# A mixture-of-experts kernel: the second expert's second matrix is split before the branch behind the routing, and part of a dense matrix is decoded beside the first products

## The chip, the cores and the metric

One core of a Trainium2 chip runs the whole program. The metric is the device time of one execution in microseconds, lower is better. The engines have one queue each and run it in order: PE (TensorE matmuls; PEld is its weight load), DVE (VectorE), ACT (ScalarE), POOL (GpSimd) and SP, which here only issues DMAs. Engines wait for each other through semaphores.

## The reference, cut to what matters

```python
x = attention(r, k, v, w, u)                    # linear attention, 3072 tokens x 384
logits = x @ w_gate                             # 8 experts, each takes exactly 384 tokens
order = argsort(-logits.flatten())              # greedy: best (token, expert) pairs first
for e in range(8):
    h = maximum(x[mask_e] @ moe_w1[e], 0)       # 384 -> 1024
    y[mask_e] = h @ moe_w2[e]                   # 1024 -> 384
h = maximum(maximum(y @ v1, y @ v2), y @ v3)    # three dense 384 x 768 matrices
out = h @ w_out                                 # 768 -> 384
```

`moe_w1`, `moe_w2` are float32 for each expert; the dense matrices `v1`, `v2`, `v3` and `w_out` come as float64 and are read as pairs of 32-bit words.

## The kernel before, in words

Three stages follow each other: the attention (until about 165 us of the profiled span), the routing (until about 197 us), and the eight experts (until the end). Every product of the experts is made from float16 halves: a matrix is split into a high and a low half, scaled by a power of two, and a product is the three passes high x high, low x high, high x low.

**Preparing a matrix** is work of ACT and DVE and is cut into small pieces. `weight(e, which)` (from line 634 on) gives the pieces of one expert matrix: four `look`s (ACT squares and sums a part of the staged matrix, line 617), `collect`, `share`, `done` (some 13 tiny DVE instructions that find the scale, lines 666, 430 to 436, 454 to 468), and five to seven `split`s (ACT writes a high half, line 684, and DVE the low half of the part before, line 688). `double(i)` (from line 707 on) gives those of a dense matrix: for each of three parts `shift`, `low`, `sign` decode float64 bits to float32 (ACT line 724, DVE lines 739, 746, 755), then the sums, `collect`, `share`, `done`, and four `split`s (ACT 780, DVE 783). `V[2]` is the third dense matrix, called V3 below, and `WO` is the last one, 384 wide.

**The planner** `Feed` holds all these pieces in one list. Under it are the stage blocks: 768 KB loads by SP into four rotating tiles (`SLOTS` is 4); `ahead()` issues a block's load when its first use is at most `AHEAD` = 6 pieces away and its tile is free. `run()` issues the next piece. `take(tag, budget)` runs pieces while its account `spare` is over 0.3; `spare` is the smaller of zero and what it was, plus the budget, and each piece run by anyone lowers it by the cost written beside the piece. A debt is kept. All of this is decided when the program is made; on the chip there are only the queues.

**Where the pieces go.** `plan()` makes the list for what remains after the attention: W2[1] (expert 1's second matrix), V3, WO, then expert 2's matrices and so on. `aside(n)` in the routing's rounds runs four pieces there, the looks of W2[1]. `settle()` ends the routing: it computes the token lists `ids` and a flag, and every engine loads the flag. `then()` issues the gather of expert 0's tokens (three indirect DMAs by POOL, line 861). Then comes a branch on every engine (`tc.If(bad != 0)`, line 1407): if the routing needs more rounds, its body runs; it doesn't here, so it is jumped over. Behind the branch the experts' PSUM and SBUF pools take over the room of the routing's pools.

`Experts.run()` (from line 1010 on) issues the experts' work in a fixed order: `gather(1)`, `first(0)` with its first five column blocks computed token slice by token slice as the gather lands (PE transposes a slice, line 886; ACT and DVE write its halves, lines 895 and 896; PE multiplies, line 904), `second(0)`, `first(1)`, `second(1)`, then for each expert `third` (six groups of three products, the dense V matrices; ACT and DVE take the maximum, lines 977 and 979) and `fourth` (WO, line 997; store by POOL, line 1002). Between products `side(time)` calls `take()` with a budget from the pieces that remain and the time until they are due; `flush(tag)` issues whatever a stage still needs, `flush(1)` V3 before `third(0)`, `flush(1.5)` WO before `fourth(0)`.

The calls around the routing's end:

```python
bad = self.settle()
then()
for _ in other:
    pass
self.aside = lambda pieces: None
with tc.If(bad != 0) as _:
```

Of the kernel before, what the change touches and what calls it, by code (L numbers as in the profile page):

```python
# [44 lines left out]
class Attention:  # L45
# [270 lines left out]
    def run(self, feed):  # L316
        nc = self.nc
        self.load(3)
        feed.ahead(2)
        for i in range(2):  # L320
            self.turn(i)
        self.scores(0)
        self.extra(0)
        for i in range(NT):
            if i == 2:
                self.routing.prepare()

            def side(j):
                if i:
                    feed.spare = 0.0  # L330
                    feed.take(9, min(0.9, feed.due((4 * (i - 1) + j) / (4 * (NT - 4)))), j)

            self.load(i + 4)
            self.across(i + 3)
            self.store(i - 1)
            self.decayed(i + 2)
            self.natural(i + 3)
            self.bonus(i + 2)
            side(1)
            self.turn(i + 2)  # L340
            self.fade(i - 1)
            side(2)
            self.scores(i + 1)
            self.extra(i + 1)
            side(3)
            self.cross(i - 1)
            self.keep(KEEP)
            self.rows(i)
            self.gate(i - 2)
            side(4)  # L350
            self.state(i)
        while feed.left(9):
            feed.run()
        self.store(NT - 1)
        self.gate(NT - 2)
        self.cross(NT - 1)
        self.gate(NT - 1)
        K = self.K
        nc.scalar.activation(K.raw, self.lg, AF.Copy, scale=-1.0)
# [137 lines left out]
class Feed:  # L497
# [30 lines left out]
    def close(self):  # L528
# [7 lines left out]
            self.items.append((tag, f, pe))  # L536
        self.plan = []

    def ahead(self, most=99):
        while self.loaded < min(most, len(self.blocks)):  # L540
            b, n = self.blocks[self.loaded], self.loaded - self.SLOTS
            free = n < 0 or self.blocks[n].last < self.at - 1
            must = b.first <= self.at
            if not must and not (free and b.first <= self.at + self.AHEAD):
                break
            b.load()
            self.loaded += 1
# [38 lines left out]
class Experts:  # L586
# [243 lines left out]
    def plan(self, late):  # L830

        feed = self.feed = Feed()
        self.early = False
        parts = [(0.2, self.weight(1, 1), None)] + [(1, self.double(i), 0) for i in late]
        parts[-1] = (1, parts[-1][1] + [(self.common, False, [], 1.5)], None)
        parts.append((1.5, self.double(3), 0))
        for e in range(2, E):
            parts += [(e, self.weight(e, 0), 7), (e + 0.3, self.weight(e, 1), 6)]
        feed.chain(parts)
        feed.close()  # L840
        feed.ahead(Feed.SLOTS)

    def open(self, ctx):
        tc = self.tc
# [65 lines left out]
            return self.psum.tile([128, CAP], F32, name="pg", bufs=3)  # L910
        return self.psum.tile([128, CAP], F32, name="ps", bufs=2)

    def first(self, e, wide=False, ahead=0):

        nc = self.nc
        h = self.act.tile([128, 2, self.KF, CAP], F16, name="ht", bufs=1)
        self.HT[e] = h
        w = self.W1[e][0]
        ps = [self.bank(f, wide) for f in range(ahead)]
        if ahead:  # L920
            for a, _ in enumerate(self.turn(e, True)):
                for f in range(ahead):
                    self.product(ps[f], w, slice(f * 128, f * 128 + 128), self.XT[e], self.KD,
                                 slice(a * 128, a * 128 + 128))
        for f in range(self.KF):
            if f < ahead:
                p = ps[f]
            else:
                p = self.bank(f, wide)
                self.product(p, w, slice(f * 128, f * 128 + 128), self.XT[e], self.KD)  # L930
            nc.scalar.activation(h[:, 0, f], p, AF.Relu)  # L931
            nc.vector.scalar_tensor_tensor(h[:, 1, f], p, 0.0, h[:, 0, f], op0=OP.max, op1=OP.subtract)  # L932
            yield
# [77 lines left out]
    def run(self):  # L1011
        nc, self.stores, feed = self.nc, [], self.feed
        F1, F2, G1, G2 = 1.45, 3.87, 4.36, 2.9
        ahead, turn = 8 * F1 + 3 * F2, 6 * G1 + 3 * G2
        clock, limit = [0.0], [1]
        room = {F1: 1.05, F2: 3.6, G1 / 3: 1.3, G2: 2.7}

        def due(tag):

            if tag < 2:  # L1020
                return ahead + 8 * F1 if tag < 1 else 2 * ahead + (6 * G1 if tag > 1 else 0.0)
            return 2 * ahead + turn + (int(tag) - 2) * (ahead + turn) + (8 * F1 + 5 * G1 if tag > int(tag) else 0.0)

        tags = sorted({item[0] for item in feed.items}, key=due)

        def side(time, part=1.0):

            clock[0] += time
            pace = max((feed.rest(tag) / max(due(tag) - clock[0] - SLACK[0] - SLACK[1] * feed.waits(tag), time) for tag in tags
                        if tag <= limit[0] and feed.left(tag)), default=0.0)  # L1030
            feed.take(limit[0], min(SLACK[2] * pace * time, part * room[time]), None, time, APART)

        def go(units, time=0):
            for _ in units:
                if time:
                    side(time)

        def flush(tag):
            while feed.rest(tag):
                feed.run()  # L1040

        self.gather(1)
        first = self.first(0, True, 5)
        for _ in range(5):
            next(first)
            clock[0] += F1
        self.gather(2)
        go(first, F1)
        go(self.turn(1))
        soon = self.second(0, lambda j: side(F2))  # L1050

        def step():
            if soon:
                soon.pop(0)()

        step()
        first = self.first(1, True)
        for f in range(self.KF):
            next(first)
            side(F1, 0.5 if soon else 1.0)  # L1060
            step()
        next(first, None)
        flush(0.2)
        soon = self.second(1, lambda j: side(F2))
        flush(1)
        limit[0] = 99
        for e in range(E):
            n = e + 1
            third, fourth = self.third(e, 0, self.KG, lambda: side(G1 / 3)), self.fourth(e)
            first = self.first(n) if e and n < E else iter(())  # L1070
            if e:
                flush(n)
            for g in range(4):
                next(third)
                step()
                side(G1 / 3, 0.6)
                if g == 1:
                    go(self.turn(e + 2))
                    self.gather(e + 3)
                for _ in range(2):  # L1080
                    if next(first, self) is not self:
                        side(F1)
            next(third)
            step()
            side(G1 / 3, 0.6)
            if e and n < E:
                flush(n + 0.3)
                soon = self.second(n, lambda j: side(F2))
                step()
            next(third)  # L1090
            step()
            side(G1 / 3, 0.6)
            flush(1.5)
            for a in range(3):
                next(fourth)
                step()
                step()
                side(G2)


class Routing:
# [291 lines left out]
    def run(self, ctx, other, aside, scales, then):  # L1393

        tc = self.tc
        self.other, self.aside = other, aside
        self.work = ctx.enter_context(tc.tile_pool(name="rwork", bufs=2))
        self.psum = ctx.enter_context(tc.tile_pool(name="psum_r", bufs=1, space=PSUM))
        scales.psum = lambda: self.psum.tile([128, 512], F32, name="px")
        for n in range(self.ROUNDS):  # L1400
            self.round(self.nl if n else self.K.raw, 6 if n == 0 else 4, n)
        bad = self.settle()
        then()
        for _ in other:
            pass
        self.aside = lambda pieces: None
        with tc.If(bad != 0) as _:
            self.more(self.MORE)
            then()
# [84 lines left out]
```

## Time and profile before

| what | value |
|---|---|
| median of the runs | 697.07 us |
| lowest and highest of three | 695.23 and 697.87 us |
| the profiled execution | 701.96 us |
| its span in the profile | 700.2 us |
| PE busy | 648.9 us, 93% |
| DVE busy | 402.0 us, 57% |
| ACT busy | 351.6 us, 50% |
| POOL busy | 238.0 us, 34% |

The span is the time from the first to the last instruction of the profiled execution. A busy share is a mean over stages with different limits; in the page's 40 slices PE is fullest from the fourteenth on, where slices of 17.5 us read 9 tenths or 8, and thinnest around the routing. The granted clock of PE is read in the same slices: 9 is full speed, 5 or 6 about half of it.

### The profile page before, as it was taken

What the parts mean: (1) busy time and instruction counts of PE and PEld (TensorE: products, weight loads), DVE (VectorE), ACT (ScalarE), POOL (GpSimd) and SP (SyncE); (2) the same over time, 40 slices, a digit from 0 to 9 for tenths busy, and PEclk for the clock granted to TensorE, in tenths of its full rate; (3) what the DMA queues carried; (4) which work ended last, traced back from release to release, by engine and by line L of the source; (5) the groups of instructions that cost most, each with busy time, mean ns of one, the idle gap of its engine ahead of it and who ended that gap; (6) DMA issues with size and microseconds to landing.
All of it is one profiled execution on the core that took longest, in us unless ns stands there. A gap on an engine that the chain in (4) does not pass through costs nothing.

```text
span 700.2 us, 14403 instructions
## 1 busy us (share of the span) xinstructions
PE 648.9 (93%) x5663; PEld 431.1 (62%) x5663; DVE 402.0 (57%) x1068; ACT 351.6 (50%) x785; POOL 238.0 (34%) x264
## 2 busy tenths in 40 slices
PE   5999998997589998699999999999999999999996
PEld 4788787886366555356666656666665666666663
DVE  7667997784734959636466544735636552551321
ACT  3576467643324645565466446545454635442321
POOL 6989999980050003123123112202212110210222
PEclk9889999996569999899999999999999999999999
DMA  7877866613033524227234410620611130000000
GB/s 226 268 230 226 276 215 199 212 47 113 2 95 67 205 90 110 94 79 141 64 124 64 141 45 35 158 91 35 157 47 69 40 96 1 35 0 1 35 1 34
DMA packets 54762, 72.97 MB, mean 104 GB/s; under 512 B 21408, under 2 KB 42016, under 8 KB 54688
## 3 DMA queue, kind: packets, MB, share of 16 engines
q1 hardware_dynamic: 51616, 62.55, 29.0%
q0 software_dynamic: 3072, 9.44, 4.9%
q8 instruction: 46, 0.75, 0.4%
q14 instruction: 28, 0.23, 0.1%
HBM read 58.41 MB, written 9.44 MB: 97 GB/s over the span
## 4 chain that ended last, share of the span: by engine, by line
PE 53%; issue 8%; DVE 5%; ACT 4%; POOL 1%; ACTq 0%; POOLq 0%; DVEq 0%
PE pg L904 25%; PE ps L904 20%; PE px L997 8%; ACT w L684 1%; DVE top L979 1%; POOL gt L984 1%; ACT junk L617 1%; DVE da L746 1%; DVE x2s L960 0%; ACT gt L983 0%; DVE ht L932 0%; DVE v L783 0%; DVE sc L430 0%; DVE da L739 0%; POOL out_dram L1002 0%
## 5 line engine op out<-in xcount | busy, mean ns | idle before, releaser
L904 PE MATMUL pg<-x2s,v 128*128 128x384 f16 x1296 | 218.2, 326 | 5.3 <-ACT top L977 3.2
L904 PEld LDWEIGHTS <-v 128*128 128x128 f16 x1296 | 126.6, 98 | 90.9 <-issue 6.0
L984 POOL TENSOR_TENSOR gt<-top,gt 128x384 f16<-128x384 f32 x48 | 44.5, 928 | 349.2 <-ACT gt L983 295.5
L904 PEld LDWEIGHTS <-w 128*128 128x128 f16 x1242 | 116.9, 99 | 75.1 <-issue 3.7
L688 DVE SCALAR_TENSOR_TENSOR w<-stage,sc,w 128x512 f16<-128x512 f32 (+1 forms) x80 | 71.6, 920 | 57.6 <-ACT w L684 57.6
L979 DVE SCALAR_TENSOR_TENSOR top<-pg,sc,top 128x384 f32<-128x384 f32 x96 | 59.0, 615 | 74.6 <-PE pg L904 63.7
L904 PE MATMUL ps<-ht,w 128*128 128x384 f16 x576 | 94.9, 326 | 1.6 <-DVE ht L932 1.6
L904 PE MATMUL ps<-xt,w 128*128 128x384 f16 (+1 forms) x540 | 88.3, 317 | 0.2 <-ACT xt L895 0.2
L997 PE MATMUL px<-wo,gt 128*128 128x384 f16 x432 | 75.0, 333 | 6.3 <-DVE wo L783 2.4
L983 ACT ACTIVATE gt<-top 128x384 f16<-128x384 f32 x48 | 25.1, 522 | 109.7 <-DVE top L979 109.7
L997 PEld LDWEIGHTS <-gt 128*128 128x128 f16 x432 | 42.7, 100 | 37.4 <-issue 7.9
L684 ACT ACTIVATE w<-stage,sc 128x512 f16<-128x512 f32 (+1 forms) x80 | 61.4, 798 | 2.2 <-DVE sc L468 2.2
L617 ACT ACTIVATE junk<-stage 128x768 bf16<-128x768 f32 x64 | 53.7, 838 | 7.2 <-DMA stage<-in_moe_w_dram 6.2
L932 DVE SCALAR_TENSOR_TENSOR ht<-ps,ht 128x384 f16<-128x384 f32 x56 | 30.9, 554 | 32.5 <-ACT ht L931 32.4
L1002 POOL DMA_INDIRECT out_dram<-o,ids x24 | 23.9, 996 | 46.0 <-ACT o L1000 46.0
L977 ACT ACTIVATE top<-pg,sc 128x384 f32<-128x384 f32 x48 | 27.6, 576 | 20.1 <-PE pg L904 17.5
L230 DVE TENSOR_TENSOR am<-pA,mask 128x512 f32<-128x512 f32 x48 | 30.7, 680 | 10.6 <-PE pA L227 10.6
L943 ACT ACTIVATE x<-ps 128x384 f32<-128x384 f32 x24 | 11.7, 490 | 46.4 <-PE ps L904 46.4
L931 ACT ACTIVATE ht<-ps 128x384 f16<-128x384 f32 x56 | 26.8, 481 | 15.7 <-PE ps L904 15.2
L227 PE MATMUL pA<-rt,kt 64*128 64x128 f32 x384 | 31.0, 297 | 2.5 <-DVE am L230 2.2
L1000 ACT ACTIVATE o<-px,sc 128x384 f32<-128x384 f32 x24 | 13.9, 580 | 38.1 <-PE px L997 34.8
L129 POOL TENSOR_TENSOR rt<-rt,tr 128x512 f32<-128x512 f32 x22 | 32.2, 1464 | 1.5 <-DMA rt<-in_rt_dram 1.5
(231 smaller groups left out, 873.6 us busy)
## 6 DMA issues: line engine op xcount, KB each, us to landing
stage<-in_moe_w_dram SPq DMA_DIRECT2D x41, 768.0 KB, 5.7
kn<-in_k_dram SPq DMA_DIRECT2D x24, 192.0 KB, 4.7
rn<-in_r_dram SPq DMA_DIRECT2D x24, 192.0 KB, 5.2
v<-in_v_dram SPq DMA_DIRECT2D x24, 192.0 KB, 3.3
rt<-in_rt_dram SPq DMA_DIRECT2D x48, 96.0 KB, 3.3
x_rows<-x SPq DMA_DIRECT2D x24, 192.0 KB, 2.6
stage<-in_moe_w_out_dram SPq DMA_DIRECT2D x3, 768.0 KB, 4.8
xg<-x_rows,ids POOLq DMA_INDIRECT x24, 4.7
```

What stands on the lines that cost most here:

```text
L129: (engine or self.nc.gpsimd).tensor_mul(self.RT[i], self.RT[i], self.tr)
L227: nc.tensor.matmul(pa[s][:, j, :], kt[FULL[s], j * C:(j + 1) * C], rt[FULL[s], j * C:(j + 1) * C], start=True, stop=True, skip_group_check ...
L230: nc.vector.tensor_mul(am[:, s], pa[s], self.mask[:, None, :].to_broadcast([128, NP, C]))
L617: self.nc.scalar.activation(self.K.junk, x, AF.Square, accum_out=total)
L684: nc.scalar.activation(hi, raw, AF.Copy, scale=st["s"])
L688: nc.vector.scalar_tensor_tensor(lo, raw, st["s"], hi, op0=OP.mult, op1=OP.subtract)
L904: nc.tensor.matmul(p[:, rows], w[:, wi, k, cols], x[:, xi, k, rows], start=k == 0 and wi + xi == 0, stop=k == kb - 1 and xi == 1, skip_gro ...
L932: nc.vector.scalar_tensor_tensor(h[:, 1, f], p, 0.0, h[:, 0, f], op0=OP.max, op1=OP.subtract)
L977: nc.scalar.activation(t, p, AF.Copy, scale=self.ratio[i])
L979: nc.vector.scalar_tensor_tensor(t, p, self.ratio[i], top, op0=OP.mult, op1=OP.max)
L984: nc.gpsimd.tensor_sub(gt[:, 1, g], top, gt[:, 0, g])
L997: nc.tensor.matmul(p, gt[:, gi, g, a * 128:(a + 1) * 128], self.WO[:, wi, g, :], start=g == 0 and gi + wi == 0, stop=g == self.KG - 1 and ...
```

## The change

Four things change.

1. In `plan()` the four first stage blocks are loaded at once (`fill()`), where `ahead()` would stop at the first block that is not needed within six pieces. Two of the four belong to V3.
2. Behind `then()`, and ahead of the branch, eight pieces run: W2[1]'s `collect`, `share`, `done` and its five `split`s.
3. In `first(0)`, `between` runs five pieces behind the second token slice's products and two behind the third's: V3's decode up to the second part's `sign`.
4. The due time by which the planner paces WO is three V groups earlier (`3 * G1` for `6 * G1`).

```diff
+    def fill(self):
+        while self.loaded < min(self.SLOTS, len(self.blocks)):
+            self.blocks[self.loaded].load()
+            self.loaded += 1
+
@@ plan
-        feed.ahead(Feed.SLOTS)
+        feed.fill()
@@ first
-    def first(self, e, wide=False, ahead=0):
+    def first(self, e, wide=False, ahead=0, between=lambda a: None):
...
                     self.product(ps[f], w, slice(f * 128, f * 128 + 128), self.XT[e], self.KD,
                                  slice(a * 128, a * 128 + 128))
+                between(a)
@@ Experts.run
-                return ahead + 8 * F1 if tag < 1 else 2 * ahead + (6 * G1 if tag > 1 else 0.0)
+                return ahead + 8 * F1 if tag < 1 else 2 * ahead + (3 * G1 if tag > 1 else 0.0)
...
-        first = self.first(0, True, 5)
+        first = self.first(0, True, 5, lambda a: self.aside((0, 5, 2)[a]))
@@ Routing.run
         for _ in other:
             pass
+        self.aside(8)
         self.aside = lambda pieces: None
         with tc.If(bad != 0) as _:
```

## Rows read from the trace of the kernel before

**Rows 1.** Page, part 1 (PE) and part 5 (the looks and sums)

```profile
PE 648.9 (93%) x5663; PEld 431.1 (62%) x5663; DVE 402.0 (57%) x1068; ACT 351.6 (50%) x785; POOL 238.0 (34%) x264
...
L617 ACT ACTIVATE junk<-stage 128x768 bf16<-128x768 f32 x64 | 53.7, 838 | 7.2 <-DMA stage<-in_moe_w_dram 6.2
```

**Rows 2.** Windows: PE, PEld, DVE, ACT, POOL busy, clock, DMA share, GB/s

```profile
280.00:300.00 20.00, 14.57 (x73) 7.59 (x71) 12.95 (x44) 10.12 (x20) 3.87 (x6) 0.83 0.23 84
```

**Rows 3.** Line 1407, the branch; durations ns min/median/max, first and last start

```profile
L1407 DVEq EVENT_SEMAPHORE  x2: 21/21/21, 200.9 to 201.0; - x2
L1407 PEldq EVENT_SEMAPHORE  x2: 51/51/51, 201.5 to 201.7; - x2
...
L1407 PEldq COMPARE_BRANCH  x1: 3648/3648/3648, 197.8 to 197.8; - x1
L1407 DVEq COMPARE_BRANCH  x1: 72/72/72, 197.9 to 197.9; - x1
```

**Rows 4.** Waits of SP, 190 to 212 us: total, times, longest

```profile
SPq L878 <- DVEq L1407: 7.9, 1, 7.9
```

**Rows 5.** Timeline from the branch to the first products: start, duration, instruction

```profile
202.13 1.51 PE L886 MATMUL px<-identf,xg 128*128 128x128 f32 x6 [1.56 <-PEq L1407]
203.16 1.09 ACT L895 ACTIVATE xt<-px,sc 128x384 f16<-128x384 f32 x2 [7.41 <-issue]
...
203.79 1.13 PE L904 MATMUL ps<-xt,w 128*128 128x128 f16 x9 [0.15 <-ACT xt L895]
...
208.56 0.27 PE L904 MATMUL pg<-xt,w 128*128 128x128 f16 x2 [1.07 <-issue]
```

**Rows 6.** Windows at the clock's two rises; the second line: PE alone

```profile
204.00:206.00 2.00, 2.00 (x24) 1.98 (x23) 0.92 (x2) 0.26 (x1) 1.60 (x2) 0.58 0.62 169
...
297.00:298.00 1.00, 1.00 (x5) 0.58 0.00 0
```

**Rows 7.** Timeline of W2[1]'s pieces, 221 to 232 us

```profile
221.24 0.15 DVE L666 TENSOR_REDUCE sc<-wpeak 128x1 f32<-128x4 f32 x1
...
223.77 0.22 DVE L468 TENSOR_SCALAR sc<-sc 128x1 int32<-128x1 int32 x2
...
227.27 3.40 ACT L684 ACTIVATE w<-stage,sc 128x768 f16<-128x768 f32 x4
228.24 3.81 DVE L688 SCALAR_TENSOR_TENSOR w<-stage,sc,w 128x768 f16<-128x768 f32 x4 [4.26 <-ACT w L684]
```

**Rows 8.** Timeline: one V3 piece on DVE, and second(1) on PE

```profile
240.64 0.95 DVE L746 SCALAR_TENSOR_TENSOR da<-stage,da 128x768 int32<-128x768 int32 x1
...
243.63 11.86 PE L904 MATMUL ps<-ht,w 128*128 128x384 f16 x72 [1.65 <-DVE ht L932]
```

**Rows 9.** Timeline: V3's scale, its splits and the first maximum

```profile
250.66 0.15 DVE L765 TENSOR_REDUCE sc<-peaks 128x1 f32<-128x3 f32 x1 [2.96 <-ACT junk L617]
...
256.38 2.58 ACT L780 ACTIVATE v<-wo,sc 128x768 f16<-128x768 f32 x3
...
260.85 0.58 ACT L977 ACTIVATE top<-pg,sc 128x384 f32<-128x384 f32 x1 [1.90 <-DVE sc L804]
```

**Rows 10.** Timeline: end of third(0), WO's scale and splits, fourth(0)

```profile
282.75 4.55 PE L904 MATMUL pg<-x2s,v 128*128 128x384 f16 x27 [0.73 <-ACT top L977]
...
287.31 0.19 DVE L434 STREAM_TRANSPOSE sc<-sc 32x32 f32<-32x32 f32 x1
...
288.46 0.21 DVE L468 TENSOR_SCALAR sc<-sc 128x1 int32<-128x1 int32 x2
...
289.63 0.32 PE L997 MATMUL px<-wo,gt 128*128 128x384 f16 x1 [2.34 <-ACT wo L780]
...
292.26 0.86 DVE L960 SCALAR_TENSOR_TENSOR x2s<-x,sc,x2s 128x384 f16<-128x384 f32 x1 [1.10 <-ACT x2s L959]
...
294.11 9.62 PE L997 MATMUL px<-wo,gt 128*128 128x384 f16 x47 [1.62 <-DVE wo L783]
...
303.56 4.55 PE L904 MATMUL pg<-x2s,v 128*128 128x384 f16 x27
```

## The prediction

> **What bounds the kernel now.** I read the page's engine line first, then windows, then the timeline around the branch and around the first dense stage. PE is busy for 93% of the span [rows 1], so an edit can only win where PE stands idle or is slow. The change touches what lies between the end of the routing and the end of fourth(0), so I looked for PE's losses there. The reader is to see five of them.
>
> (a) The branch. PE's compare-branch starts at 197.8 and takes 3.65 us; DVE's starts at 197.9, and DVE's next instruction comes at 200.9 [rows 3]. ACT, PE and DVE do nothing for the experts before 202.13, when PE transposes the first token slices; products start at 203.79 [rows 5].
> (b) Inside the first products PE stops once more: the last two matmuls of slice 0 come at 208.56 behind 1.07 us of "issue" [rows 5], a stop in which nothing is waited for. With the gaps before it I count 1.5 us.
> (c) Before second(1) PE waits 1.65 us for DVE's half of the activations [rows 8]; DVE is there decoding V3 between the activations, one `low` being 0.95 us [rows 8].
> (d) second(1) ends at 243.63 + 11.86 = 255.5 [rows 8]. The first maximum of third(0) on ACT can start at 260.85 only, since V3's splits run from 256.38 and `common`, which gives it its scale, follows them [rows 9]. PE has three PSUM tiles here, so its second group can't start before 260.85 + 0.58 = 261.43. The 27 matmuls of a group are 27 x 0.165 = 4.5 us (11.86 / 72 = 0.165 each [rows 8]); 261.43 - 255.5 - 4.5 = 1.5 us lost.
> (e) The other five groups run from 261.43 to 282.75 + 4.55 = 287.3 [rows 10]: 25.9 us for 135 x 0.165 = 22.3, so 3.6 lost, to DVE's and ACT's queues. Then WO isn't ready: PE has one matmul at 289.63, its bulk at 294.11, and fourth(0) ends at 303.56 [rows 10]: 16.3 us for 54 x 0.165 = 8.9, so 7.4 lost. Of that a part is the clock, a mean of 0.83 in 280 to 300 us [rows 2].
>
> Everything there is to win in the touched stretch is (b) to (e), some 15.7 us.
>
> **Part 1, four stage tiles at once.** Two more loads of 768 KB on SP's queue in the routing. No product of the routing waits for a load, and W2[1]'s own blocks stay ahead of them in the queue. V3's third block follows when W2[1]'s first tile is free, about 203.5 by the times below, beside the landing gathers; the products wait longer than that for another reason. Nothing gained by itself, nothing lost.
>
> **Part 2, W2[1] ahead of the branch.** Eight pieces leave second(0), where PE ran on without a stop, so nothing is gained there. Where they go they stand between the flag's load and the branch on ACT and DVE. DVE would have branched at 197.9 [rows 3]. Instead: `collect`, `share`, `done` take 221.24 to 223.99 = 2.75 us [rows 7], until 200.65. ACT's four high halves take 3.40 [rows 7], until 204.1. DVE's low halves follow ACT's by 0.97 (228.24 - 227.27) and take 3.81 [rows 7], so the last starts at 200.7 + 0.97 + 3 x 0.95 = 204.5 and ends at 205.5. A sequencer can pass to the branch when it has given out the last one, so DVE branches at 204.5, not 197.9. Between its branch and its next instruction lay 200.9 - 197.9 - 0.07 = 2.9 us [rows 3]; with the same again DVE is behind the branch at 207.5 instead of 201.0, 6.5 later.
>
> Who waits for that? SP's next instruction waited 7.9 us for DVE to be behind the branch [rows 4], though SP itself had nothing to do with DVE. ACT sat idle 7.4 us until 203.16 [rows 5]. The code says why: the experts' pools take over the routing's PSUM and SBUF, so the first user of each waits for every engine to be out of the routing, the branch included. I take it that PE's transposes wait too. In before PE was itself behind the branch only at 201.7 [rows 3], so DVE's 201.0 was hidden; at 207.5 it is not. From DVE's exit to the products I keep the distance from PE's exit, 203.79 - 201.7 = 2.1, less some 0.2 that PE's own exit took: products at about 209.4, **5.6 us later**. Bounds: 3.6 if DVE pays nothing at the branch, 0.9 if PE and ACT need not wait for DVE at all (then the ACT halves end at 204.1 instead of the 203.16 at which ACT's transposed slice was due).
>
> The Trainium skill (Runtime: NRT & Kernel Launch, Instruction fetch mechanics) says that a taken branch to a target outside the engine's instruction window has to fetch that page before it can go on. The 2.9 us on DVE and 3.65 on PE agree with it; by this rule the 2.9 are paid again, behind the moved pieces, and the products start at 209.4; without it they would start at 207.4.
>
> **What the later start gives back and takes.** Loss (b) looks like PE running dry of instructions soon after the branch; with 5.6 us of waiting it has time to have them: -1.5 (bounds -1.6 and 0). The clock: PE worked at half speed from 203.79 until it rose within 204 to 206, at about 205.7 (a mean of 0.58) [rows 6], with a burst of warming matmuls until shortly before. Now PE stands idle some 7 us first. The nearest row is the restart at 294.11 [rows 10], which reached full speed within 297 to 298 [rows 6], 3.7 us later. So 3.7 us at half speed for 1.9: **+0.9** (bounds 0 and 2.5).
>
> **Part 3, V3's decode beside the products.** Between the second and third slice's halves DVE gets five pieces, three of them with 0.95-like DVE instructions and two of about 0.55: some 3.0 us. PE has two slices of 45 narrow matmuls to do meanwhile, about 0.06 us each, 5 us with the transposes, so the third slice's low half is there in time: 0 (at worst +1). What it takes away is (c): during first(1) DVE has only activations and second(0)'s scale: **-1.65** (0 at worst).
>
> But the planner's account decides when the rest of V3 runs. Following `spare` through `run()` and `take()`: in before it stands at -3.6 when the experts start (four looks of 0.9). Now it stands there with a further -7.1 (W2[1]'s eight pieces) and -6.3 (V3's seven), at **-17.0**. The budgets are the same or smaller (0.5 to 0.6 for each unit of first(0), 1.8 to 2.7 for each of second(0), 0.5 to 1.05 in first(1)), and bring it to -2.8 at the end of first(1). So nothing at all is issued in second(0) and first(1), and V3's third part resumes only with second(1)'s first product, as late as in before. There it costs one step: `collect` (at 250.66 in before [rows 9]) and `done` go behind second(1)'s third product instead of its second, and all four splits into flush(1). In time: ACT's last two sums of V3, 0.84 and 0.2 each [rows 1], stand behind the second product's evacuation (4 us before the stage's end, 24 x 0.165, plus 0.9); then 2.75 for the scale. That is 4.0 - 0.9 - 2.1 - 2.75 = 1.75 past the end of second(1); in before the splits began 256.38 - 255.5 = 0.9 past it [rows 8, 9]. **+0.9** (bounds 0 and 1.5).
>
> **Part 4, WO due earlier.** The earlier due time raises the pace, but the budget of a V product is capped (1.3, and 0.78 at a group's end), and flush(1) leaves a debt of 4.1 where it left 1.5. Following the account, WO's first piece runs in third(0)'s second group, not its first; its `collect` in the sixth, not the fifth; `done` and all splits in flush(1.5), where in before two splits stood inside the sixth group. So WO's chain is **later**, not earlier. Inside third(0) the DVE pieces are spread a little more evenly: -0.5 (bounds -2 and +1). At its end E, DVE has the last maximum, ACT the cast, and second(1)'s third halving passes ACT and DVE (0.6 to 0.9 each; 0.86 for DVE's [rows 10]): some 2.8 us; then `share` and `done`, 287.31 to 288.67 = 1.35 [rows 10], then the first high half, 0.95. First matmul at E + 5.1, where it was 289.63 - 287.3 = 2.3. The third low half, which the last 6 of 18 matmuls of the first tile need, is there at about E + 8.1, where PE's bulk had started at E + 6.8: later by 0.4 in effect, and the clock falls for as long as before: **+0.7** (bounds -0.5 and +2.5).
>
> **The sum.** +5.6 - 1.5 + 0.9 - 1.65 + 0.9 - 0.5 + 0.7 = +4.45. From expert 1's third on the order is the same but for a piece or two and PE sets the pace, so this lag stays. Against the profiled execution, 701.96: 706.4. That execution stood 4.9 above the median of the runs shown, so for the median: 697.07 + 4.45 = **701.5**.
>
> **Rivals.** R1, the branch is cheap on DVE this time: exit at 205.5, start +3.6, the sum +2.4, 699.5. For it: the branch instruction itself is 0.07 us on DVE; against: the 2.9 behind it [rows 3]. R2, nobody waits for DVE's exit: start +0.9, the fetch stop (b) stays, the clock as before: +0.9 - 1.65 + 0.9 - 0.5 + 0.7 = +0.35, 697.4. Against it: rows 4 and 5. R3, on the faster side: with DVE free of V3 and W2[1], third(0) and WO lose their stops, if WO's `done` comes before the end of third(0); then 3.6 and some 7 of 7.4 go: 4.45 + 0.5 - 0.7 - 10.6 = -6.3, 690.7. Against it: the account above. R4, slower still: WO's later start takes the clock for twice as long and (b) stays: +4.45 + 1.5 + 2.5, 705.5.
>
> **How the numbers follow.** Forecast 0.62, R1 0.12, R2 0.10, R3 0.07, R4 0.09. The range reaches from under R2 to R4: 697.0 to 705.5, leaving out R3 and the ends. A measurement tells 0.5%, 3.5 us, from no change: slower means over 700.6. The forecast's own range is 699.5 to 703.5, so some 0.50 of its 0.62 is slower, with R4 0.09 and a little of R1; the rest of these and R2 is no change.
>
> **What would show it.** In the profile of the changed kernel: DVE's compare-branch at about 204.5 and its exit about 3 us later; the transposes right behind that exit; products at about 209.4; no wait for DVE before second(1); ACT's V3 splits about 1.8 us past second(1); WO's first matmul about 5 us past third(0). It is wrong if the transposes start before DVE's exit, or if fourth(0) starts without a wait.

## The result and the profile after

The changed kernel takes 705.4 us (median of four runs, 704.3 to 706.4) beside 697.5 us for the kernel before: a ratio of 1.0118 with a 95% interval of 1.0100 to 1.0136. Run again later beside other runs of before it gave 704.9 us and 1.0093 (1.0062 to 1.0125). The prediction was 701.5 with 697.0 to 705.5: slower as forecast, but by 8 us where 4.45 had been summed.

The span of its profiled execution is 702.8 us, that of before 700.2, only 2.6 apart. The two executions differ already ahead of the change: the first gather is issued at 197.23 in before and at 193.51 after. A second trace of the kernel before (below) has it at 193.27, so 197.23 was that execution's, not the kernel's. So I count from the gather's issue. Two rows of before's timeline (start, duration, instruction) are needed for it:

```profile
197.23 1.17 POOL L861 DMA_INDIRECT xg<-x_rows,ids  x1 [3.10 <-POOLq L1407]
...
218.42 11.86 PE L904 MATMUL ps<-ht,w 128*128 128x384 f16 x72
```

The same stretch after, in the timeline (start, duration, instruction, idle before it and who ended it). Line numbers have moved by five to seven:

```profile
193.51 1.17 POOL L866 DMA_INDIRECT xg<-x_rows,ids  x1 [3.08 <-POOLq L1414]
...
196.96 3.41 ACT L689 ACTIVATE w<-stage,sc 128x768 f16<-128x768 f32 x4 [4.92 <-DVE sc L468]
197.93 3.81 DVE L693 SCALAR_TENSOR_TENSOR w<-stage,sc,w 128x768 f16<-128x768 f32 x4 [0.94 <-ACT w L689]
199.90 0.33 SPq L614 DMA_DIRECT2D stage<-in_moe_w_dram  x1
205.48 1.51 PE L891 MATMUL px<-identf,xg 128*128 128x128 f32 x6 [9.37 <-DVEq L1414]
205.54 0.94 POOL L866 DMA_INDIRECT xg<-x_rows,ids  x1 [8.35 <-DVEq L1414]
...
207.15 1.13 PE L909 MATMUL ps<-xt,w 128*128 128x128 f16 x9 [0.15 <-ACT xt L900]
...
211.35 0.50 PE L891 MATMUL px<-identf,xg 128*128 128x128 f32 x3
...
221.10 11.86 PE L909 MATMUL ps<-ht,w 128*128 128x384 f16 x72
```

PE's transposes now wait 9.37 us for "DVEq L1414", which is DVE leaving the branch, and POOL's second gather, that of expert 1's tokens, 8.35 for the same. In before PE's wait there was for its own branch [rows 5]. The branch's own rows, by queue (durations in ns, then the starts of the first and the last):

```profile
L1414 PEldq EVENT_SEMAPHORE  x2: 51/51/51, 198.0 to 198.1; - x2
L1414 ACTq EVENT_SEMAPHORE  x2: 17/17/17, 200.4 to 200.5; - x2
L1414 DVEq EVENT_SEMAPHORE  x2: 21/21/21, 205.3 to 205.4; - x2
...
L1414 PEldq COMPARE_BRANCH  x1: 3765/3765/3765, 194.2 to 194.2; - x1
L1414 ACTq COMPARE_BRANCH  x1: 50/50/50, 197.0 to 197.0; - x1
...
L1414 DVEq COMPARE_BRANCH  x1: 72/72/72, 200.4 to 200.4; - x1
```

PE is out at 198.1, ACT at 200.5, DVE at 205.4. DVE branches at 200.4, while its last low half is still to run, and its next instruction comes 4.9 us later, at 205.3. In before the two were 197.9 and 200.9, 3.0 apart [rows 3].

What follows in the timeline of after, to the end of fourth(0):

```profile
244.50 11.86 PE L909 MATMUL ps<-ht,w 128*128 128x384 f16 x72
...
258.15 2.59 ACT L785 ACTIVATE v<-wo,sc 128x768 f16<-128x768 f32 x3 [0.79 <-DVE sc L468]
...
262.63 0.58 ACT L983 ACTIVATE top<-pg,sc 128x384 f32<-128x384 f32 x1 [1.89 <-DVE sc L809]
...
284.04 3.09 PE L909 MATMUL pg<-x2s,v 128*128 128x384 f16 x18 [0.21 <-DVE top L985]
...
284.52 0.84 ACT L622 ACTIVATE junk<-stage 128x768 bf16<-128x768 f32 x1
...
285.49 0.84 ACT L622 ACTIVATE junk<-stage 128x768 bf16<-128x768 f32 x1
...
287.25 0.56 ACT L983 ACTIVATE top<-pg,sc 128x384 f32<-128x384 f32 x1
...
288.69 0.14 DVE L770 TENSOR_REDUCE sc<-peaks 128x1 f32<-128x3 f32 x1
...
289.95 0.60 DVE L985 SCALAR_TENSOR_TENSOR top<-pg,sc,top 128x384 f32<-128x384 f32 x1
...
293.58 0.21 DVE L468 TENSOR_SCALAR sc<-sc 128x1 int32<-128x1 int32 x2
...
294.75 0.48 PE L1003 MATMUL px<-wo,gt 128*128 128x384 f16 x1 [7.62 <-ACT wo L785]
...
306.19 4.55 PE L909 MATMUL pg<-x2s,v 128*128 128x384 f16 x27
```

The windows of 20 us (columns as in [rows 2]) show the last part as the thin one, with PE busy for 11.8 of 20 us and a mean clock of 0.74, where the same 284 to 304 us of before had 15.3 and 0.83:

```profile
264.00:284.00 20.00, 18.90 (x114) 10.93 (x113) 17.22 (x37) 10.62 (x20) 7.32 (x7) 1.00 0.59 169
284.00:304.00 20.00, 11.76 (x59) 6.35 (x59) 11.66 (x42) 10.24 (x20) 2.95 (x5) 0.74 0.18 59
```

Taken apart from these rows and [rows 5, 8, 9, 10], each distance in us (third(0) ends at 287.3 before, at 284.04 + 3.09 = 287.1 after):

| from, to | before | after | difference | forecast |
|---|---|---|---|---|
| gather's issue, first products | 6.6 | 13.6 | +7.1 | +5.6 |
| first products, second(0) | 14.6 | 13.95 | -0.7 | -0.6 |
| second(0), second(1) | 25.2 | 23.4 | -1.8 | -1.65 |
| second(1), first maximum of third(0) | 17.2 | 18.1 | +0.9 | +0.9 |
| first maximum, end of third(0) | 26.45 | 24.5 | -1.95 | -0.5 |
| end of third(0), end of fourth(0) | 16.3 | 19.1 | +2.8 | +0.7 |
| end of fourth(0), end of the span | 396.6 | 396.6 | 0 | 0 |
| sum | 503.0 | 509.3 | +6.3 | +4.45 |

### The profile page after: what moved, and what is told of

Its sections match the earlier page's. It is cut to its first block, busy times and chain, and to the rows that moved or that the text cites. A ratio compares the mean times of both kernels' runs of the same rounds, so it can differ in the third digit from the quotient of the medians.

```text
span 702.8 us, 14405 instructions
## 1 busy us (share of the span) xinstructions
PE 644.3 (92%) x5663; PEld 427.9 (61%) x5663; DVE 398.7 (57%) x1068; ACT 352.8 (50%) x785; POOL 238.7 (34%) x264
## 4 chain that ended last, share of the span: by engine, by line
PE 55%; issue 8%; DVE 3%; ACT 3%; POOL 1%; POOLq 0%; DVEq 0%; ACTq 0%
PE pg L909 26%; PE ps L909 21%; PE px L1003 8%; DVE top L985 1%; ACT junk L622 1%; POOL gt L990 1%; ACT w L689 1%; ACT gt L989 0%; DVE v L788 0%; DVE gt L760 0%; POOL out_dram L1008 0%; DVE da L744 0%; ACT x2s L965 0%; DVE sc L430 0%; ACT top L983 0%
## 5 line engine op out<-in xcount | busy, mean ns | idle before, releaser
L949 ACT ACTIVATE x<-ps 128x384 f32<-128x384 f32 x24 | 11.8, 492 | 49.7 <-PE ps L909 49.7
L866 POOL DMA_INDIRECT xg<-x_rows,ids x24 | 25.3, 1055 | 17.4 <-DVEq L1414 8.4
```

## The experiments

Theory A: the loss is the branch. The eight pieces keep DVE from branching, and every engine's first work behind the branch waits for DVE. The main rival: the pieces' new order and the planner's account behind the branch.

**The eight pieces alone.** Added to the kernel before:

```diff
         for _ in other:
             pass
+        self.aside(8)
         self.aside = lambda pieces: None
```

> The kernel before with one edit: W2[1]'s eight pieces run behind the first gather, ahead of the branch; nothing else of the change. Theory A (the branch): everything behind the branch waits for DVE's exit, and DVE branches only when it has given out its last low half. From the first gather's issue to the first products 6.6 us become some 13 to 14, as in the changed kernel (13.6), and the time goes from about 697 to 703 or 705. Rival B (the pieces' order and the planner's account behind the branch make the loss, not the branch): the distance stays under 8 us and the time under 699.5.

Measured: 702.8 us, ratio 1.0092 (1.0065 to 1.0118). The gather is issued at 194.08, and the transposes come 12.1 us later, held as in the changed kernel, as two rows of its timeline show:

```profile
194.08 1.17 POOL L861 DMA_INDIRECT xg<-x_rows,ids  x1 [3.10 <-POOLq L1408]
...
206.14 1.51 PE L886 MATMUL px<-identf,xg 128*128 128x128 f32 x6 [9.14 <-DVEq L1408]
```

So this one line brings a loss of 6.4 us (697 x 0.0092) by itself.

**Everything but the eight pieces.** The changed kernel without `self.aside(8)`. The list of pieces keeps its order, so the seven pieces beside the first products are here W2[1]'s scale and first splits, not V3's decode:

> The changed kernel without the eight pieces ahead of the branch; the seven pieces beside the first products, the four early loads and the earlier due time stay, so the seven pieces are now W2[1]'s scale and first splits. Theory A (the branch): the gather-to-products distance is back at 6.6 us (13.6 in the changed kernel) and the time falls by 5 to 8 us, to 697 to 700. Rival B (order and account): the distance may shrink, but the time stays above 702.

Measured: 696.8 us, ratio 0.9998 (0.9980 to 1.0015). The loss is gone; transposes follow the gather by 5.1 us, and the wait ahead of them is again for PE's own branch, in its timeline:

```profile
194.17 1.17 POOL L866 DMA_INDIRECT xg<-x_rows,ids  x1 [3.10 <-POOLq L1413]
...
199.26 0.94 PE L891 MATMUL px<-identf,xg 128*128 128x128 f32 x6 [2.20 <-PEq L1413]
```

The eight pieces alone make most of the loss, and the rest of the change without them makes none: theory A is shown, and the main rival falls as the cause of the bulk. No run takes the branch itself away, so what the pieces would cost at that place without it isn't known. The run also says that the rest of the change, with these seven pieces beside the first products, is worth nothing that can be measured as it stands.

**Why 4.9 us from DVE's branch to its next instruction, and not 3.0?** Five kernels look at this. First, the program issues no load while the eight pieces run, so that V3's third block comes behind the branch in SP's queue:

```diff
+        self.feed.hold = True
         self.aside(8)
+        self.feed.hold = False
...
     def run(self):
-        self.ahead()
+        if not self.hold:
+            self.ahead()
```

> The changed kernel, except that no stage load is issued while the eight pieces run; V3's third block is loaded behind the branch. In the changed kernel DVE's exit came 4.9 us after its branch, where it was 3.0 in the kernel before. Theory C (the load, 768 KB issued at 199.9 us, just ahead of DVE's branch at 200.4, holds up DVE's next instructions): the distance from branch to exit is back at about 3.0 us and the products start some 1.9 us earlier. Rival D (the place in the code or chance decides): it stays at 4 to 5 us.

Its branch rows, and SP's row of its timeline:

```profile
L1419 DVEq EVENT_SEMAPHORE  x2: 21/21/21, 205.2 to 205.3; - x2
L1419 SPq COMPARE_BRANCH  x1: 53/53/53, 188.6 to 188.6; - x1
...
L1419 DVEq COMPARE_BRANCH  x1: 72/72/72, 200.2 to 200.2; - x1
```

```profile
199.70 0.34 SPq L617 DMA_DIRECT2D stage<-in_moe_w_dram  x1
```

Measured: 704.2 us, ratio 1.0104 (1.0079 to 1.0129); branch at 200.2, next instruction at 205.2, 5.0 apart. This does not settle theory C. On the chip the load did not move: SP was through its own branch 11 us before and issued the load as soon as W2[1]'s first tile was free, at 199.70, which is 0.5 us ahead of DVE's branch, just as in the changed kernel (199.90 and 200.4). Next, the first three pieces alone (`self.aside(3)` in the kernel before):

> The kernel before with the first three of W2[1]'s pieces ahead of the branch: thirteen short DVE instructions, 2.75 us, and none on ACT. Theory A (dose): DVE's last one ends some 3.5 us behind the gather's issue, its exit comes at 6.5 (3.8 in before, 11.9 with eight pieces) and the products at 8.3 (6.6 and 13.7). Branch to exit stays at 3.0 us here if the 5.0 us with eight pieces came of the number of instructions or of the work still running on DVE when it branches; it is 5.0 if any piece ahead of the branch is enough. Rival: the exit stays at 3.8, since these pieces fit into the fetch's shadow.

DVE's rows of the branch:

```profile
L1408 DVEq EVENT_SEMAPHORE  x2: 21/21/21, 201.1 to 201.2; - x2
...
L1408 DVEq COMPARE_BRANCH  x1: 72/72/72, 198.0 to 198.0; - x1
```

Measured: 198.0 and 201.1, 3.1 apart; products 7.85 us behind the gather (202.61 less 194.76). The rival that the pieces fit into the shadow falls: 2.75 us of DVE work moved DVE's exit by 2.7, and the products by 1.3, since PE's own exit hides a part. (The single time, 702.0 us, has a drop of the clock around second(1), to a mean of 0.91 in 240 to 260 us, and isn't used.) Then one long DVE instruction:

```diff
+        long = self.small("long", [128, 32])
+        self.nc.vector.tensor_reduce(long, self.K.onesf[:, None, :].to_broadcast([128, 32, 128]), AX.X, OP.add)
         self.aside = lambda pieces: None
```

> The kernel before with one more DVE instruction ahead of the branch, a reduction of 4096 elements whose result nobody reads, some 4.3 us. Theory G (drain): DVE's sequencer reaches the branch while the instruction still runs, and the next instructions come only some 3 us after its end: exit some 8 us behind the gather's issue, branch to exit 6 to 7 us. Rival H (code position: the 5.0 us of the eight pieces came of their 37 instructions): branch to exit 3 to 4.5 us, exit no later than the end of the long instruction plus 0.3, at about 5.

DVE's row of it in the timeline:

```profile
192.98 4.42 DVE L1407 TENSOR_REDUCE long<-onesf 128x32 f32<-128x4096 f32 x1 [1.01 <-POOLq L1409]
```

And DVE's rows of the branch in the same kernel:

```profile
L1409 DVEq EVENT_SEMAPHORE  x2: 21/21/21, 197.4 to 197.5; - x2
...
L1409 DVEq COMPARE_BRANCH  x1: 72/72/72, 193.0 to 193.0; - x1
```

Measured: DVE branches at 193.0, as the instruction starts, and is out at 197.4, as it ends (192.98 + 4.42); products 7.1 us behind the gather, 0.6 later than in before, 696.8 us. So the theory that the branch's 4.9 us starts only when DVE's work ends (G) falls: what DVE needs behind a branch goes on while an instruction given out earlier still runs. It also says what makes the eight pieces dear. DVE's work there is 6.6 us (2.75 + 3.81); with 4.42 us costing the products 0.6, I estimate that a good part of it would have been hidden as one instruction. Each piece waits for the one before or for ACT, and as I read it the sequencer has to stand at each of them before it can get to the branch.

Then as many DVE instructions as in the eight pieces, by three pieces and eight one-element memsets:

```diff
+        self.aside(3)
+        pad = self.small("pad", [1, 1])
+        for _ in range(8):
+            self.nc.vector.memset(pad, 0.0)
```

> The kernel before with W2[1]'s first three pieces ahead of the branch, as in the run where branch to exit stayed at 3.2 us, and eight more one-element memsets on DVE, so that as many DVE instructions stand ahead of the branch as with all eight pieces, but nothing on ACT and no load. Theory H (the number of instructions ahead of the branch decides): branch to exit 5.0 us as with the eight pieces. Rival (ACT's pieces or the semaphores between ACT and DVE do): it stays at 3.2.

DVE's rows of the branch:

```profile
L1411 DVEq EVENT_SEMAPHORE  x2: 21/21/21, 200.0 to 200.1; - x2
...
L1411 DVEq COMPARE_BRANCH  x1: 72/72/72, 196.9 to 196.9; - x1
```

Measured: 196.9 and 200.0, 3.1 apart; products 9.3 us behind the gather, a single time of 700.3 us. So the theory that the number of DVE instructions ahead of the branch makes it (H) falls too. Last, the scale and ACT's four high halves ahead of the branch, DVE's low halves and the loads behind it:

> The kernel before with W2[1]'s scale (13 DVE instructions) and the four high halves on ACT ahead of the branch; the four low halves on DVE and all loads come behind it. So DVE branches at 3.3 us behind the gather's issue and ACT has its four pieces ahead of its own branch. Theory A: DVE's exit at 6.5, as with the scale alone, ACT's at 7.0; products at 8.3 to 9 instead of 13.7, and the time 2 to 4 us above before instead of 6.4. If ACT's pieces are what makes DVE's branch to exit 5.0 us instead of 3.1, it is 5 here and DVE's exit comes at 8.2; if it is the low halves, or the later moment, it stays at 3.2.

From its timeline:

```profile
200.40 0.94 POOL L867 DMA_INDIRECT xg<-x_rows,ids  x1 [2.89 <-DVEq L1419]
200.42 3.81 DVE L692 SCALAR_TENSOR_TENSOR w<-stage,sc,w 128x768 f16<-128x768 f32 x4 [3.11 <-DVEq L1419]
200.79 1.54 PE L892 MATMUL px<-identf,xg 128*128 128x128 f32 x6 [3.62 <-ACTq L1419]
```

Measured: 700.8 us, ratio 1.0049 (1.0027 to 1.0072); products 8.65 us behind the gather (202.49 less 193.84). DVE's idle before its low halves is the 3.1 us, and PE is now held by ACT (ACTq), whose first instruction behind the branch came as its high halves ended at 200.7. Moving the low halves and the loads behind the branch gives back some 3 of the 6.4 us, by two ratios whose intervals overlap a little (1.0065 and 1.0072).

What makes the 4.9 is narrowed, not settled: it isn't the number of DVE instructions, work running on DVE, or ACT's pieces. Two things are left, and the five traces with 4.9 to 5.0 us have both of them: the low halves ahead of the branch, and the 768 KB load for which the second low half frees the tile. In these five the load's packets move behind DVE's branch, until 3.1 to 3.4 us after it. None of the eight traces with 2.9 to 3.4 us has a load there, but for the kernel before without debt (below), where one ends 0.9 us after the branch; its distance is the 3.4. The packets of q14, an instruction queue in the page's DMA part, tell the same: the first behind DVE's branch starts 0.9 to 1.3 us after it in the other nine traces, and 2.6 to 3.1 us after it in the five, within the last 0.7 us of the load. From that packet to DVE's next instruction it is 1.9 us in eleven of the fourteen, on either side, so the extra time lies ahead of the packet. So theory C, the load, is the likely one. It is not shown: no run has the eight pieces ahead of the branch without a load beside it, and the profile doesn't say for which engine a packet of q14 is.

**The planner's account.** The changed kernel, with pieces run by hand not charged:

```diff
     def aside(self, pieces):
+        spare = self.feed.spare
         for _ in range(pieces):
             self.feed.run()
+        self.feed.spare = spare
```

> The changed kernel, except that the pieces run by hand (in the routing, ahead of the branch, beside the first products) are not charged to the planner's account. By the planner's arithmetic V3's scale is then ready in first(1), its splits end with second(1)'s first product, and WO's pieces start with third(0)'s first product. Theory E (the debt keeps V3 and WO late): no wait for V3's splits at the head of third(0), 1.5 to 2.5 us less there, WO's scale about one product earlier and fourth(0)'s wait of 7.6 us down to 3 to 5, in all 3 to 5 us faster than the changed kernel, while gather-to-products stays at 13.6. Rival F (DVE's load, not the order, sets third(0)'s end): under 1.5 us.

Measured: 701.2 us, ratio 1.0071 (1.0048 to 1.0095), some 1.5 to 3.3 us less than the changed kernel's two ratios give (697 x (1.0093 - 1.0071) and 697 x (1.0118 - 1.0071)). That lies between the two forecasts, under 1.5 and 3 to 5; all four times (701.05 to 702.43) are under all eight of the changed kernel (703.55 to 706.47). From its timeline:

```profile
256.03 13.33 PE L911 MATMUL pg<-x2s,v 128*128 128x384 f16 x81
257.69 0.58 ACT L985 ACTIVATE top<-pg,sc 128x384 f32<-128x384 f32 x1 [0.50 <-PE pg L911]
...
282.34 6.12 PE L911 MATMUL pg<-x2s,v 128*128 128x384 f16 x27 [3.42 <-ACT top L985]
...
289.23 0.32 PE L1005 MATMUL px<-wo,gt 128*128 128x384 f16 x1 [0.77 <-ACT wo L785]
...
302.97 4.55 PE L911 MATMUL pg<-x2s,v 128*128 128x384 f16 x27
```

The debt is real: without it the first maximum waits only for PE, and fourth(0) 0.77 us instead of 7.62. Part of it third(0) takes back, with 3.42 us of waiting for ACT in the middle. So the account costs, as the one theory had it, and its stops return in third(0), as the other had it.

**Both together**, no pieces ahead of the branch and no debt:

> The changed kernel without the pieces ahead of the branch, and with the pieces run by hand not charged to the planner's account. Theory A and E together: gather to products 6.4 us as without the eight pieces, and WO's scale a product earlier, so fourth(0) waits under 1 us; some 3 us faster than the kernel before, 692 to 695 us. Rival: third(0) gives back on DVE what fourth(0) wins, and the time is within 1 us of before.

Measured: 692.2 us, ratio 0.9930 (0.9914 to 0.9947): the fastest kernel of this study, 4.9 us under before (697 x 0.0070). It differs from the run without the eight pieces, 0.9998 (0.9980 to 1.0015), by the account alone, so here the account is worth the whole 0.7%. From its timeline:

```profile
254.45 0.58 ACT L985 ACTIVATE top<-pg,sc 128x384 f32<-128x384 f32 x1
...
275.78 5.91 PE L911 MATMUL pg<-x2s,v 128*128 128x384 f16 x27 [4.48 <-ACT top L985]
...
282.67 0.32 PE L1005 MATMUL px<-wo,gt 128*128 128x384 f16 x1 [0.98 <-ACT wo L785]
```

Third(0) still loses 4.5 us to ACT, so there may be more to win. **The account alone**, the same edit in the kernel before:

> The kernel before with the one edit of the account: pieces run by hand (here the four looks in the routing) are not charged. Question: is the gain of the version without the pieces ahead of the branch and without debt (0.993) the account's alone, or does V3's decode beside the first products carry part of it. Account alone: 0.993 to 0.996, WO's scale earlier and fourth(0) waiting about 1 us instead of 2.4 plus the slow clock. Otherwise: within 0.3% of before.

Measured: 694.7 us, ratio 0.9960 (0.9943 to 0.9977). So the account is worth 0.4% in the kernel before, where the edit frees only the four looks. With the rest of the change, where it also frees the seven pieces beside the first products, it is worth 0.7%. The upper end of the one interval, 0.9947, stands just over the lower end of the other, 0.9943: that the rest of the change adds anything, once it isn't charged, is likely, not shown. V3's decode is no part of this, since it stands beside the first products only in the kernels that have the eight pieces too.

**The two kernels once more.**

> The kernel before once more, to have a second trace of it. The profiled execution of before lay 4.5 us above the median of its runs. If that came from ahead of the gather, the gather's issue is now at about 193.5 us (197.2 there) and what lies behind it 503 us again; if from behind it, the rest is 500 to 501 us, and so much more is the loss of the change against a usual execution of before.

Measured: gather at 193.27, span 695.8, so 502.5 us behind the gather (503.0 in the first trace). Of the 4.5 us by which the profiled execution of before stood above its median, 4.0 came from ahead of the gather (197.23 less 193.27).

> The changed kernel once more, beside runs of before on the same chip. Its traces' difference to before behind the gather is 6.3 us, the medians' difference 8. If the rest is the granted clock, runs with a lower mean clock are longer in proportion, and the profiled one shows a longer stretch at half clock behind the branch or before fourth(0); the ratio is again 1.010 to 1.0136.

Measured: 704.9 us, ratio 1.0093 (1.0062 to 1.0125); gather at 193.21, span 702.7: 509.5 behind the gather. Against 502.5 and 503.0 that is +6.5 to +7.0, near the ratio's 6.5.

## Why the prediction was right and wrong

**Right: the direction, and the reason.** DVE's branch was forecast 6.6 us behind its place in before (197.9 to 204.5); it came 6.2 later, counted from the gather (0.7 us behind it in before, 6.9 after). PE's transposes stand right behind DVE's exit. That everything waits for it is shown by the pair of runs with and without the eight pieces. R1 (a cheap branch) and R2 (nobody waits) fall with the same rows. R3 (third(0) and WO lose their stops) did not happen in the changed kernel; in the version without debt a part of it did. R4 (slower still, by WO's later start and the clock) happened by half: WO did start later and the clock stayed low longer, but PE's stop inside the first products, (b), which R4 kept, went. That R4's 705.5 lies beside the measured 705.4 is luck, since 1.5 of it is that stop.

**Right in size, in part by luck:** the lost stop (b) and the longer time at half clock, together -0.7 for -0.6. Both had been read from one execution. The second trace of before has no such stop, and PE stood there at half clock for 4.7 us from its first product, not for 1.9 (a granted clock of 0.50 from 199.75 to 204, and of 0.57 in 204.0 to 204.5); in the changed kernel it was 3.5. Against that trace the stretch is 0.5 shorter all the same (14.47 to 13.95).

**Right in size:** the wait before second(1), -1.8 for -1.65 (243.63 had a wait, 244.50 has none); V3's splits one step later, +0.9 for +0.9 (they start 258.15 - 256.4 = 1.8 us past second(1)). DVE's 3.0 us for the five pieces is right too (0.56 + 0.96 + 0.96 + 0.55 in the changed kernel), though from four DVE instructions; the first of the five pieces is ACT's alone. The account at -17 fits the order, and the run without debt shows that it costs.

**Wrong, the first term.** "With the same again" was the step that failed: I took DVE's 2.9 us between branch and next instruction for a constant. From start to start it was 2.9 to 3.4 in eight traces, and 4.9 to 5.0 in the five that carry all eight pieces ahead of the branch. DVE's exit came 8.1 us later where 6.5 had been forecast, and the term measured 7.1 where 5.6 was summed. The likely reason is one that I had in hand and put at nothing: Part 1 let V3's third block start at about 203.5, with DVE's branch forecast for 204.5, and called it "nothing lost". The traces have that load beside the branch wherever the distance is long; that it is the cause stays open. The Trainium skill (Runtime: NRT & Kernel Launch, Instruction fetch mechanics) tells of the fetch behind a taken branch, which the traces agree with, as none of DVE's instructions behind its branch comes within 2.9 us of it; it gives no time for it.

**Wrong, the last term.** Third(0) and fourth(0) were summed at +0.2 and came to +0.85. My E, PE's end of third(0), was taken for the time at which DVE has its last maximum. It ran at 289.95, 2.8 later: ACT's last maximum came only at 287.25, behind two looks of expert 2's matrix (284.52 and 285.49), and DVE had WO's `collect` (from 288.69) in front of its own. PE ended third(0) 1.95 us earlier than before, counted from the first maximum, and then had nothing to do: first matmul at E + 7.6, not E + 5.1, and a longer time at the lower clock (0.74 in that window).

**Wrong, the base.** With these two terms as measured, the sum of 4.45 becomes the 6.3 of the traces, but the timed runs differ by 6.5 (697 x 0.0093) to 8.2 (697 x 0.0118). Up to 2 us of the first comparison lie outside the two traces; of its four runs of the changed kernel two had a mean granted clock of 0.941 with 706.3 to 706.4 us, and two 0.948 to 0.949 with 704.3 to 704.5. No trace exists of the former, so where in the kernel that lies is not known.

## What to carry to other kernels

Work that "fills a wait" must be looked at for what stands behind it in its queue: here a branch, and behind the branch a place where each engine waits for all others. Ahead of such a place a chain of small dependent instructions was dear here, and one long independent instruction cheap: 6.6 us of DVE work in eight pieces put the products off by 7.1 us, and 4.42 us in one instruction by 0.6. And where a planner keeps an account, work pulled forward by hand should not be charged to it, or the planner pays for the gift with later work; leaving the charge out won 0.2 to 0.7% in three kernels. And an edit that moves an issue in the program has to be looked up in the trace: the load put behind the branch was issued at the same moment as without the edit, since SP's queue was long past the branch and issued it when its tile came free.

## What was not expected of the hardware

DVE's distance from its compare-branch to the next instruction lies about two values here, 2.9 to 3.4 and 4.9 to 5.0 us; PE's branch lasts 3.57 to 3.85 us in the fourteen traces. The other engines hardly pay: in before ACT goes on 0.5 us after its branch (196.4 and 196.9), SP 0.5 (192.5 and 193.0) and POOL 0.2 (197.0 and 197.2). DVE's time goes on while the engine runs what it was given before: the 4.42 us reduction ran from DVE's branch to its exit and cost the products 0.6 us. ACT's 3.4 us in the changed kernel, from 197.0 to 200.4, is another thing: its four halves run from 196.96 for 3.41 us, and its next instruction comes as they end.
